# Moving the denominators' transfers to GpSimd, loading values last, and forming key-value sums directly as feature by value

## Chip, cores and metric

The kernel runs on one core of one Trainium2 chip. The metric is the device time of one execution in microseconds (us); lower is better. Three runs of the kernel before gave 923.36, 926.24 and 926.26 us, a median of 926.24 us.

## What is computed

The reference chains three parts; all data are float32 (some weights arrive as float64 words and are converted on the chip).

```python
def phi(x):                       # x: 4 batches, 8 heads, 576 tokens, 64 wide
    proj = x @ w_phi              # 128 features
    proj = proj - max(abs(proj), axis=-1)
    return concat(exp(proj), exp(-proj))
q_p, k_p = phi(q), phi(k)
kv  = einsum('bhsf,bhsd->bhfd', k_p, v)
z   = sum(k_p, axis=s)
out = einsum('bhsf,bhfd->bhsd', q_p, kv) / (einsum('bhsf,bhf->bhs', q_p, z) + 1e-6)
x = out as 2304 tokens x 512
h = max(x @ w1, x @ w2, x @ w3)   # 512 -> 768
y = h @ w_out                     # 768 -> 512
t = y @ w_in                      # 512 -> 2048
g = max(t, 0) + alpha * min(t, 0)
return g @ w_out2                 # 2048 -> 512
```

## The kernel before, in words

**Stages.** Heads are handled in pairs, 4 pairs a batch, 16 in all; pair number i counts through the batches. `keys(pair)` (L255) projects the keys, forms `e` = exp of both signs, and sums keys times values over five token tiles into one PSUM bank `kvp`. The values come with a block of ones between the two heads (`v`, shaped 5 x 3 x 64), so numerators and denominators come out of one product. `queries(pair)` (L313) projects the queries, transposes them, takes exp, multiplies by the pair's sums (`pn`), and copies numerator and denominator to `nd`. Then (L363 to L387) eight transfers a pair handle the denominators: two gather a denominator row into `dc` (64 partitions by 9), one moves the second head's numerators under the first's (`nd<-nd`), one writes the reciprocals to DRAM (`r_d`), four read them back broadcast (`xr<-r_d`). The product `xr` is split into a high and a low part (`xh`, `xl`), as every operand of the later matrix products is: a product is formed as three matmuls, high*high, high*low, low*high. For the first batch GpSimd does the multiply, the copy and the subtraction (L379 to L386); for others VectorE and ScalarE do.

**Plain pairs.** For the first two batches (8 pairs, `plain_kv`) the key-value sum is a plain float32 matmul, which the trace shows as two records each. It is formed value by feature: `rv` (128 columns) is loaded as weights and `e` streams 256 columns, so 10 matmuls a pair. The result is copied to `kvs` by ScalarE (L295), turned by four transposes on TensorE (L298) into `kvt`, and copied again to `kvf` (L301).

**Layer 1** (`layer1`, L398) works in units of one batch half (288 tokens) by 128 outputs: 36 matmuls, then ScalarE and VectorE take the maximum of three banks into `ho`, which goes to DRAM as `h_d` (L417). Units are placed between the pairs: unit number u0 = 3 * (i - 4) - LAG at pair i (L443), so that they fill TensorE during the attention; what is left runs after it (L538). `split_w123` converts their weights on VectorE and ScalarE (L153).

**Layer 2** (L548 to L563) reads `h_d` chunk by chunk (`load_h`, L516, tile `hr`) and writes `y_d` by way of `yo` (L560, two buffers). **Layer 3** (L608 to L634) reads `y_d`, writes `g_d`. **The last stage** (L642 to L683) goes through 9 blocks of 256 tokens, two halves each. It uses a seven-product scheme: `left(block, half)` (L582) reads `g_d` into `a`, forms four sums `s`, and makes seven factors `o` (high part by ScalarE, low part by L602: every second one on GpSimd except in the first block's first half, the others on VectorE). 168 matmuls a block take them in `ORDER`.

**What sets the order.** Each engine and each DMA queue works strictly in the order in which its instructions were laid down. That order comes from a planner that runs through a simulated timeline when the kernel is built, with the priorities that `tc.high_priority` gives. The loads of q, k, v and tails (L144), the staging of weights (L173, L468), the eight denominator transfers (L366, L367, L371, L378) and `h_d` of the first three batches all share SyncE's queue (SP); an instruction there that waits for a semaphore holds up those behind it. `g_d`, and `h_d` of the last batch, go by GpSimd's queue (POOL), `y_d` by ScalarE's.

Of the kernel before, what the change touches and what calls it, by code (L numbers as in the profile page):

```python
# [10 lines left out]
F32 = mybir.dt.float32  # L11
# [8 lines left out]
P = 128  # L20
# [13 lines left out]
CHUNKS = ((0, 2 * P), (2 * P, S - 2 * P))  # L34
EPS = 1e-6
XBUFS = (6, 6)
LAG = 1
PLAIN = 5
CONVERT_IN = (2, 1, 2, 1, 3, 3, 3, 3)
SOON, NOW, LATER, LAST = 400, 1000, -100, -200  # L40
# [11 lines left out]
def tile_kernel(ctx: ExitStack, tc: tile.TileContext, qT, kT, tails, v, w_phi, w1, w2, w3, w_out, w_in, w_out2, alpha, out):  # L52
# [82 lines left out]
    def load_pair(pair):  # L135

        odd = pair[1] % 2
        tags = ["xh", "rv", "rt", "xl"] if plain(pair) else ["raw", "rv", "rt", "raw"]
        if plain_kv(pair):
            tags[1] = ("vl", "vh")[odd]  # L140
        shapes = ([P, SM], [P, 5, 3, D], [P, 2 * ST], [P, SM])
        for what, tag, shape, src in zip("kvtq", tags, shapes, (kT, v, tails, qT)):
            t = ap.tile(shape, F32, tag=tag, bufs=2 if tag in ("raw", "xh", "xl") else 1, name=what)
            nc.sync.dma_start(t, src[pair])  # L144
            raws[pair, what] = t

    def plain(pair):
        return pair[0] * NPAIR + pair[1] < PLAIN

    def plain_kv(pair):  # L150
        return pair[0] < 2
# [103 lines left out]
    def keys(pair):  # L255

        rv = raws[pair, "v"]
        if not plain_kv(pair):
            if not vs:
                vs.extend(ap.tile([P, 5, 3, D], F32R, tag=tag, bufs=1, name=tag) for tag in ("vh", "vl"))  # L260
                part = slice(None)
            else:
                part = slice(None, None, 2)
            vh, vl = vs
            hi_act(vh[:, :, part], rv[:, :, part])
            sub(V, vl[:, :, part], rv[:, :, part], vh[:, :, part])
        kvp = bank("kv", 1, "kvp")
        first = True
        for tiles, e in exp_keys(pair):
            n = len(tiles) * 512  # L270
            if plain_kv(pair):
                ops = ((rv, e),)
            else:
                kh = ap.tile([P, 1024], F32R, tag="kh", bufs=2, name="kh")
                kl = ap.tile([P, 1024], F32R, tag="kl", bufs=2, name="kl")
                hi_act(kh[:, :n], e[:, :n])
                sub(V, kl[:, :n], e[:, :n], kh[:, :n])
                ops = ((vh, kh), (vl, kh), (vh, kl))
            yield
            for i, t in enumerate(tiles):  # L280
                for h in range(2):
                    c = slice(i * 512 + h * 256, i * 512 + h * 256 + 256)
                    for x, y in ops:
                        nc.tensor.matmul(  # L284
                            kvp[:, h * 256 : h * 256 + 256],
                            x[:, t, h : h + 2].rearrange("p a d -> p (a d)"),
                            y[:, c],
                            start=first,
                            stop=t == 4 and y is ops[-1][1],
                            skip_group_check=True,  # L290
                        )
                        first = False
        yield
        kvs = ap.tile([P, 512], F32, tag="kvs", bufs=1, name="kvs")
        A.activation(kvs, kvp, AF.Copy)  # L295
        kvt = bank("p1", 3, "kvt") if pair[0] == 0 else bank("kv", 1, "kvt")
        for i in range(4):
            nc.tensor.transpose(kvt[:, i * P : (i + 1) * P], kvs[:, i * P : (i + 1) * P], ident)  # L298
        if plain_kv(pair):
            kvf = ap.tile([P, 2, 2, P], F32, tag=("kvh", "kvl")[pair[1] % 2], bufs=2, name="kvf")  # L300
            A.activation(kvf.rearrange("p a b c -> p (a b c)"), kvt, AF.Copy)  # L301
            kvs_of[pair] = (kvf,)
            return
        kvh = ap.tile([P, 2, 2, P], F32R, tag="kvh", bufs=2, name="kvh")
        kvl = ap.tile([P, 2, 2, P], F32R, tag="kvl", bufs=2, name="kvl")
        hi_act(kvh.rearrange("p a b c -> p (a b c)"), kvt)
        sub(V, kvl.rearrange("p a b c -> p (a b c)"), kvt, kvh.rearrange("p a b c -> p (a b c)"))
        kvs_of[pair] = (kvh, kvl)
# [4 lines left out]
    def queries(pair):  # L313
# [49 lines left out]
        dc = ap.tile([P, S // D], F32, tag="dc", bufs=2, name="dc")  # L363
        for h in range(2):
            dr = D * (1 - h)
            nc.sync.dma_start(dc[h * D : (h + 1) * D], nd[h][dr : dr + 1].rearrange("a (p n) -> a p n", p=D))  # L366
        nc.sync.dma_start(nd[0][D:], nd[1][D:])  # L367
        V.tensor_scalar(dc, dc, EPS, None, op0=ALU.add)
        V.reciprocal(dc, dc)
        rows = r_d[pair[0], pair[1]]  # L370
        nc.sync.dma_start(rows.rearrange("h (p n) -> (h p) n", p=D), dc)  # L371
        res = []
        for c in range(2):
            cs = slice(c * CH, (c + 1) * CH)
            xr = raw_tile()
            for h in range(2):
                r = slice(h * D, (h + 1) * D)
                nc.sync.dma_start(xr[r], rows[h : h + 1, cs].to_broadcast([D, CH]))  # L378
            e = G if pair[0] == 0 else V  # L379
            e.tensor_tensor(xr, nd[0][:, cs], xr, op=ALU.mult)  # L380
            xh, xl = x_tiles(c)
            if pair[0] == 0:
                G.tensor_copy(xh, xr)  # L383
            else:
                hi_act(xh, xr)
            sub(e, xl, xr, xh)  # L386
            res.append((xh, xl))  # L387
# [10 lines left out]
    def layer1(b, c, f, x, w, spread=False):  # L398
        pw = []
        for j in range(3):  # L400
            if spread:
                p = bank(("pn", "pt", "kv")[j], 1, "p1")
            else:
                p = bank("p1", 3, "p1")
            ops = []
            for k in range(KT):
                ks = slice(k * P, (k + 1) * P)
                ops += three(w[j][:, 0, ks], w[j][:, 1, ks], *x[k][c])
            products(p[:, :CH], ops)
            pw.append(p)  # L410
        s1 = xp.tile([P, CH], F32, tag="s1", bufs=2, name="s1")
        A.activation(s1, pw[0][:, :CH], AF.Copy)
        V.tensor_tensor(s1, pw[1][:, :CH], s1, op=ALU.max)
        ho = xp.tile([P, CH], F32, tag="ho", bufs=2, name="ho")
        V.tensor_tensor(ho, pw[2][:, :CH], s1, op=ALU.max)  # L415
        o = b * S + c * CH
        (nc.gpsimd if b == B - 1 else nc.sync).dma_start(h_d[f, :, o : o + CH], ho)  # L417

    pairs = [(b, pr) for b in range(B) for pr in range(NPAIR)]
    xs = {b: [] for b in range(B)}  # L420
# [94 lines left out]

    def load_h(c, k):  # L516
        hh, hl = x_tiles(max(c % 2, k // XBUFS[0]))
        pool, tag, bufs = ((xp, "xr", 3), (xp, "xr", 3), (xp, "s1", 2), (gp, "neg", 2))[(2 * c + k) % 4]
        if c == 0:
            pool, tag, bufs = xp, "xr", 3  # L520
        hr = pool.tile([P, CH], F32, tag=tag, bufs=bufs, name="hr")
        nc.sync.dma_start(hr, h_d[k, :, c * CH : (c + 1) * CH])
        hi_act(hh, hr)
        sub(V, hl, hr, hh)
        hs[c, k] = (hh, hl)
# [22 lines left out]
    for c in range(2 * B):  # L548
# [5 lines left out]
        for m in range(KT):  # L554
            ms = slice(m * P, (m + 1) * P)
            ops = []
            for k in range(NF1):
                ops += three(wo[k][:, 0, ms], wo[k][:, 1, ms], *hs[c, k])
            products(p2[m][:, :CH], ops)
            yo = xp.tile([P, CH], F32, tag="ho", bufs=2, name="yo")  # L560
            A.activation(yo, p2[m][:, :CH], AF.Copy)
            nc.scalar.dma_start(y_d[m, :, t0 : t0 + CH], yo)
        convert(2)  # L563
# [13 lines left out]
    T = P  # L577
# [4 lines left out]
    def left(block, half):  # L582

        ready[block, half] = res = {}
        a = []
        for kh in range(2):
            t = ap4.tile([P, 4, 2 * T], F32, tag="a", bufs=4, name="a")
            r = slice(kh * 8 + half * 4, kh * 8 + half * 4 + 4)
            nc.sync.dma_start(t, g_d[r, :, block * 2 * T : (block + 1) * 2 * T].rearrange("f p n -> p f n"))
            a.append(t)  # L590
        (a00, a10), (a01, a11) = ((t[:, :, :T], t[:, :, T:]) for t in a)
        s1, s2, s3, s4 = (ap4.tile([P, 4, T], F32, tag="s", bufs=4, name="s") for _ in range(4))
        V.tensor_tensor(s3, a00, a10, op=ALU.subtract)
        V.tensor_tensor(s1, a10, a11, op=ALU.add)
        V.tensor_tensor(s2, s1, a00, op=ALU.subtract)
        V.tensor_tensor(s4, a01, s2, op=ALU.subtract)  # L596
        for n, i in enumerate(ORDER):
            src = (a00, a01, s4, a11, s1, s2, s3)[i]
            o = op4.tile([P, 2, 512], F32R, name="o") if half else ring2.tile([P, 2, 512], F32R, tag="w", name="o")
            ov = o.rearrange("p a (f n) -> p a f n", f=4)  # L600
            hi_act(ov[:, 0], src)
            sub(G if n % 2 and block + half else V, ov[:, 1], src, ov[:, 0])  # L602
            res[i] = o
            yield

    V.tensor_scalar(al, al, -1.0, 1.0, op0=ALU.mult, op1=ALU.add)
    load_y(0, 0)
# [129 lines left out]
```

## Time and profile before

| what | before |
|---|---|
| median of 3 runs | 926.24 us (923.36 to 926.26) |
| the profiled execution's own time | 925.09 us |
| its span, first to last instruction | 923.3 us |
| TensorE matmul busy | 899.8 us (97%), 6689 matmul records |
| VectorE busy | 642.5 us (70%) |
| ScalarE busy | 468.2 us (51%) |
| GpSimd busy | 173.5 us (19%) |
| mean granted TensorE clock | 0.997 |

In the profile's rows PE is TensorE's matmuls, PEld its weight loads, DVE VectorE, ACT ScalarE, POOL GpSimd and SP SyncE; SPq, POOLq and ACTq are these engines' DMA issues. A name like `p<-xh,w123t` says which tile is written from which. L253 and L74 are lines of helpers that all products and all low-part subtractions share. Matmul ends are modelled, so that overlapping matmuls count as busy while nothing is lost between them; starts are recorded.

### The profile page before, as it was taken

Reading aid. Unit: us, or ns where it says so; the run is one execution under the profiler, and the core shown is the slowest. Engines: PE = TensorE matmul, PEld = TensorE weight load, DVE = VectorE, ACT = ScalarE, POOL = GpSimd, SP = SyncE. Lnnn points to the kernel's source line nnn. Section 1 sums busy time; section 2 is a strip of 40 time slices with the busy share of each in tenths; the row PEclk is TensorE's granted clock in tenths of the full one; section 3 lists DMA queues with packets and bytes.
Section 4 is the critical chain, followed back from the end, with each engine's and each line's share of the span. In section 5 each row is a group of like instructions: output and inputs, shape, how many; then the busy total and the mean of one; then the engine's idle time right before and its main releaser. Section 6 shows DMA issues by size and latency. Waiting matters only on the chain.

```text
span 923.3 us, 18029 instructions
## 1 busy us (share of the span) xinstructions
PE 899.8 (97%) x6689; PEld 876.6 (95%) x6689; DVE 642.5 (70%) x1239; ACT 468.2 (51%) x1084; POOL 173.5 (19%) x221
## 2 busy tenths in 40 slices
PE   8987999999999999999999999999999998999998
PEld 7866899999999999999999999999999998999998
DVE  6998556788887632889889294447443598878881
ACT  5867556777777521444466363335333353444440
POOL 0032100000000000001000023333333363444440
PEclk9999999999999999999999999999999999999999
DMA  9664323222331112766678555445542345443421
GB/s 318 195 193 143 84 59 81 74 80 82 104 95 44 31 58 65 225 184 213 203 231 248 185 171 167 131 147 175 193 149 100 111 116 156 135 141 116 138 69 46
DMA packets 83159, 125.98 MB, mean 136 GB/s; under 512 B 14208, under 2 KB 61952, under 8 KB 83072
## 3 DMA queue, kind: packets, MB, share of 16 engines
q1 hardware_dynamic: 71744, 99.47, 36.4%
q0 software_dynamic: 6720, 20.65, 6.2%
q10 hardware_dynamic: 4608, 4.72, 1.5%
q8 instruction: 52, 0.85, 0.4%
q14 instruction: 35, 0.29, 0.1%
HBM read 86.91 MB, written 35.46 MB: 133 GB/s over the span
## 4 chain that ended last, share of the span: by engine, by line
PE 73%; DVE 11%; DMA 8%; issue 3%; ACT 2%; SPq 0%; POOL 0%; ACTq 0%; DVEq 0%; POOLq 0%
PE p L253 43%; PE acc L656 12%; PE kvp L284 6%; PE pn L253 5%; PE pj L253 5%; DVE o L74 2%; DMA st<-in_w_out 2%; DMA y_d<-yo 2%; PE pt L346 2%; DMA hr<-h_d 1%; DVE wt L87 1%; DVE wt L89 1%; ACT o L68 1%; DVE xl L74 1%; DVE s L596 1%
## 5 line engine op out<-in xcount | busy, mean ns | idle before, releaser
L253 PE MATMUL p<-xh,w123t 128*128 128x288 f32 x1152 | 242.3, 298 | 3.2 <-POOL xh L383 3.1
L253 PE MATMUL p<-xh,wi 128*128 128x288 f32 x1024 | 203.9, 296 | 1.2 <-DVE g L627 1.2
L253 PEld LDWEIGHTS p<-xh,w123t 128*128 128x128 f32 x1152 | 187.1, 188 | 4.8 <-POOL xh L383 3.5
L656 PE MATMUL acc<-wq,o 128*128 128x256 f32 x1512 | 182.0, 282 | 3.6 <-DVE o L74 3.2
L656 PEld LDWEIGHTS acc<-wq,o 128*128 128x128 f32 x1512 | 179.9, 190 | 5.6 <-DVE o L74 5.1
L253 PE MATMUL p<-xl,w123t 128*128 128x288 f32 x576 | 171.4, 298 | 0.0
L253 PEld LDWEIGHTS p<-xh,wi 128*128 128x128 f32 x1024 | 163.2, 188 | 1.5 <-DVE g L627 1.5
L253 PE MATMUL p<-xl,wi 128*128 128x288 f32 x512 | 149.5, 293 | 0.0
L253 PEld LDWEIGHTS p<-xl,w123t 128*128 128x128 f32 x576 | 108.2, 188 | 0.6
L628 POOL DMA_DIRECT2D g_d<-g x128 | 69.5, 544 | 208.5 <-DVE g L627 204.6
L627 DVE SCALAR_TENSOR_TENSOR g<-neg,al,p 128x288 f32<-128x288 f32 x128 | 64.3, 511 | 63.7 <-ACT neg L625 63.3
L253 PEld LDWEIGHTS p<-xl,wi 128*128 128x128 f32 x512 | 97.0, 190 | 0.0
L625 ACT ACTIVATE neg<-p 128x288 f32<-128x288 f32 x128 | 51.2, 407 | 84.9 <-PE p L253 81.0
L253 PE MATMUL p<-xh,wo 128*128 128x288 f32 x384 | 76.9, 296 | 0.8 <-ACT xh L68 0.7
L417 POOL DMA_DIRECT2D h_d<-ho x12 | 6.7, 555 | 354.7 <-DVE ho L415 354.7
L68 ACT ACTIVATE o<-s 128x512 fp32r<-128x512 f32 x72 | 44.3, 629 | 55.1 <-PE acc L656 29.6
L74 DVE TENSOR_TENSOR xl<-xr,xh 128x288 fp32r<-128x288 f32 x88 | 38.8, 455 | 37.2 <-ACT xh L68 32.2
L68 ACT ACTIVATE xh<-xr 128x288 fp32r<-128x288 f32 x88 | 37.8, 444 | 49.5 <-DMA xr<-y_d 34.3
L253 PEld LDWEIGHTS p<-xh,wo 128*128 128x128 f32 x384 | 61.1, 188 | 1.3 <-ACT xh L68 1.3
L74 POOL TENSOR_TENSOR o<-s,o 128x512 fp32r<-128x512 f32 x34 | 49.3, 1453 | 65.1 <-ACT o L68 65.1
L204 DVE TENSOR_REDUCE mx<-pj 128x4 f32<-128x512 f32 (+1 forms) x80 | 49.8, 627 | 10.6 <-PE pj L253 10.5
L253 PE MATMUL p<-xl,wo 128*128 128x288 f32 x192 | 56.3, 293 | 0.5 <-DVE xl L74 0.3
(138 smaller groups left out, 1632.3 us busy)
## 6 DMA issues: line engine op xcount, KB each, us to landing
g_d<-g POOLq DMA_DIRECT2D x128, 144.0 KB, 2.1
a<-g_d SPq DMA_DIRECT2D x36, 512.0 KB, 3.8
st<-in_w_out SPq DMA_DIRECT2D x22, 512.0 KB, 4.4
wst<-in_w SPq DMA_DIRECT2D x18, 512.0 KB, 5.6
xr<-y_d SPq DMA_DIRECT2D x64, 144.0 KB, 2.4
st<-in_w_in SPq DMA_DIRECT2D x16, 512.0 KB, 3.8
v<-in_v SPq DMA_DIRECT2D x16, 480.0 KB, 4.2
hr<-h_d SPq DMA_DIRECT2D x48, 144.0 KB, 3.9
```

Of the source, the lines that this page charges most:

```text
L68: A.activation(dst, src, AF.Copy)
L74: eng.tensor_tensor(dst, src, hi.bitcast(F32), op=ALU.subtract)
L87: V.scalar_tensor_tensor(wu, low, 29, wu, op0=ALU.logical_shift_right, op1=ALU.bitwise_or)
L89: V.scalar_tensor_tensor(wu, high, 0xC0000000, wu, op0=ALU.bitwise_and, op1=ALU.bitwise_or)
L204: V.tensor_reduce(mx, pv, axis=AX.X, op=ALU.max, apply_absolute_value=True, negate=True)
L253: nc.tensor.matmul(dst, x, y, start=i == 0, stop=i == len(ops) - 1, **kw)
L284: nc.tensor.matmul(kvp[:, h * 256 : h * 256 + 256], x[:, t, h : h + 2].rearrange("p a d -> p (a d)"), y[:, c], start=first, stop=t == 4 an ...
L346: nc.tensor.transpose(pt[:, c : c + P], pp[:, 2 * i + h], ident)
L625: A.activation(neg, p, AF.Relu, scale=-1.0)
L627: V.scalar_tensor_tensor(g, neg, al[:, f : f + 1], p, op0=ALU.mult, op1=ALU.add)
L628: nc.gpsimd.dma_start(g_d[f, :, c * CH : (c + 1) * CH], g)
L656: nc.tensor.matmul(acc[i], x, y, start=half == 0 and f == 0 and n == 0 and PLACE[i][1] == 0, stop=half == 1 and f == 3 and n == 2, skip_gr ...
```

## The change

`LAG` goes from 1 to 2. From the second pair on, a pair's loads go out in the order keys, tails, queries, values (before: keys, values, tails, queries). The eight denominator transfers and all `h_d` writes go by GpSimd's queue. The fourth pair's multiply and split go from GpSimd to VectorE and ScalarE. For the 8 plain pairs the key-value sum is formed feature by value: `e` is the weights, `rv` streams 128 columns, 20 matmuls a pair instead of 10, and the first copy and the transposes go away. `hr` uses the tags `xr` and `s1` alone (before also `neg`), `yo` uses `ho` and `neg` in turn (four buffers instead of two). In the last stage both halves of `a` are one tile, the sums `s` are formed between the factors instead of ahead of them, and every low part is made by VectorE.

```diff
-LAG = 1
+LAG = 2
...
-        for what, tag, shape, src in zip("kvtq", tags, shapes, (kT, v, tails, qT)):
+        for what, tag, shape, src in sorted(zip("kvtq", tags, shapes, (kT, v, tails, qT)), key=lambda x: ("ktqv" if i_of(pair) else "kvtq").index(x[0])):
...
-            for i, t in enumerate(tiles):
+            for i, t in enumerate(tiles if plain_kv(pair) else ()):
+                for j in range(4):
+                    c = slice(i * 512 + j * P, i * 512 + j * P + P)
+                    nc.tensor.matmul(
+                        kvp[:, j * P : (j + 1) * P],
+                        e[:, c],
+                        rv[:, t, j // 2 : j // 2 + 2].rearrange("p a d -> p (a d)"),
+                        start=first,
+                        stop=t == 4,
+                        skip_group_check=True,
+                    )
+                    first = False
+            for i, t in enumerate(() if plain_kv(pair) else tiles):
...
+        if plain_kv(pair):
+            kvf = ap.tile([P, 2, 2, P], F32, tag=("kvh", "kvl")[pair[1] % 2], bufs=2, name="kvf")
+            A.activation(kvf.rearrange("p a b c -> p (a b c)"), kvp, AF.Copy)
+            kvs_of[pair] = (kvf,)
+            return
         kvs = ap.tile([P, 512], F32, tag="kvs", bufs=1, name="kvs")
         A.activation(kvs, kvp, AF.Copy)
...
-            nc.sync.dma_start(dc[h * D : (h + 1) * D], nd[h][dr : dr + 1].rearrange("a (p n) -> a p n", p=D))
-        nc.sync.dma_start(nd[0][D:], nd[1][D:])
+            nc.gpsimd.dma_start(dc[h * D : (h + 1) * D], nd[h][dr : dr + 1].rearrange("a (p n) -> a p n", p=D))
+        nc.gpsimd.dma_start(nd[0][D:], nd[1][D:])
...
-        nc.sync.dma_start(rows.rearrange("h (p n) -> (h p) n", p=D), dc)
+        nc.gpsimd.dma_start(rows.rearrange("h (p n) -> (h p) n", p=D), dc)
...
-                nc.sync.dma_start(xr[r], rows[h : h + 1, cs].to_broadcast([D, CH]))
-            e = G if pair[0] == 0 else V
+                nc.gpsimd.dma_start(xr[r], rows[h : h + 1, cs].to_broadcast([D, CH]))
+            e = G if i_of(pair) < NPAIR - 1 else V
...
-        (nc.gpsimd if b == B - 1 else nc.sync).dma_start(h_d[f, :, o : o + CH], ho)
+        nc.gpsimd.dma_start(h_d[f, :, o : o + CH], ho)
...
-        pool, tag, bufs = ((xp, "xr", 3), (xp, "xr", 3), (xp, "s1", 2), (gp, "neg", 2))[(2 * c + k) % 4]
-        if c == 0:
-            pool, tag, bufs = xp, "xr", 3
+        tag, bufs = ("s1", 2) if c and k % 2 else ("xr", 3)
...
-            yo = xp.tile([P, CH], F32, tag="ho", bufs=2, name="yo")
+            pool, tag = ((xp, "ho"), (gp, "neg"))[m % 2]
+            yo = pool.tile([P, CH], F32, tag=tag, bufs=2, name="yo")
...
-            sub(G if n % 2 and block + half else V, ov[:, 1], src, ov[:, 0])
+            sub(V, ov[:, 1], src, ov[:, 0])
```

In `left` the new order is: factor 0, sums s1 and s2, factor 5, sum s3, factors 6, 4, 1, 3, sum s4, factor 2.

## Rows read from the trace of the kernel before

**Rows 1.** Busy time by stage: stretch, its length, then each engine's busy us.
```profile
core 0: us, PE busy (x) PEld busy (x) DVE busy (x) ACT busy (x) POOL busy (x), PEclk, DMA share, GB/s
0.00:100.00 100.00, 86.96 (x432) 72.19 (x433) 84.03 (x174) 68.00 (x159) 20.43 (x30) 1.00 0.63 199
100.00:360.00 260.00, 259.92 (x1966) 255.36 (x1965) 173.89 (x355) 158.15 (x408) 0.00 (x0) 1.00 0.26 72
...
460.00:540.00 80.00, 77.46 (x575) 76.11 (x575) 57.68 (x122) 46.11 (x113) 1.25 (x2) 1.00 0.69 213
...
735.00:770.00 35.00, 31.71 (x251) 30.90 (x250) 29.22 (x38) 15.64 (x29) 15.87 (x11) 0.95 0.48 139
770.00:904.00 134.00, 133.67 (x1127) 132.45 (x1126) 108.72 (x154) 61.17 (x102) 61.24 (x41) 1.00 0.40 119
```

**Rows 2.** Waits of PE in the first 100 us: total us, times, longest.
```profile
PE p L253 <- POOL xh L383: 3.1, 1, 3.1
PE pj L253 <- ACT ke L235: 3.0, 2, 2.7
```

**Rows 3.** Waits of DVE in the first 100 us.
```profile
DVE xht L71 <- DMA t<-in_tails: 3.4, 1, 3.4
DVE dc L368 <- DMA dc<-nd: 2.0, 1, 2.0
```

**Rows 4.** SP's issues in order of time: start, us, line, transfer.
```profile
69.53 1.10 SPq L378 DMA_DIRECT2D xr<-r_d  x2
70.68 0.58 SPq L144 DMA_DIRECT2D t<-in_tails  x1
```

**Rows 5.** Waits of the SP queue, 8 to 100 us.
```profile
SPq L378 <- DMA r_d<-dc: 12.3, 4, 4.2
```

**Rows 6.** POOL in order of time: first and last instruction of the fourth pair.
```profile
91.40 1.59 POOL L380 TENSOR_TENSOR xr<-nd,xr 128x288 f32<-128x288 f32 x1 [12.33 <-DMA xr<-r_d]
...
95.44 0.81 POOL L74 TENSOR_TENSOR xl<-xr,xh 128x288 fp32r<-128x288 f32 x1
```

**Rows 7.** The chain of waits, second plain pair: start, us, engine, tile, records.
```profile
31.51 0.44 PE kvt L298 x4
31.95 1.73 PE kvp L284 x8
```

**Rows 8.** Weight loads of the plain products, all: count, busy us, mean ns.
```profile
L284 PEld LDWEIGHTS kvp<-ke,v 128*128 128x128 f32 x160 | 29.6, 192 | 5.9 <-ACT ke L228 1.8 <-ACT ke L235 0.2
```

**Rows 9.** Idle time ahead of the instructions that touch yo: until what, us, times.
```profile
  DMA y_d<-yo: 19.2, 11
```

**Rows 10.** Waits of PE from 450 to 545 us.
```profile
PE p L253 <- DVE g L627: 1.2, 1, 1.2
```

**Rows 11.** A transfer's count, KB and us to landing.
```profile
hr<-h_d SPq DMA_DIRECT2D x48, 144.0 KB, 3.9
```

**Rows 12.** Waits of PE from 735 to 790 us.
```profile
PE acc L656 <- DVE o L74: 3.2, 2, 2.9
```

**Rows 13.** Groups from 785 to 885 us (five blocks): count, busy us, mean ns.
```profile
L74 POOL TENSOR_TENSOR o<-s,o 128x512 fp32r<-128x512 f32 x20 | 28.6, 1432 | 36.5 <-ACT o L68 36.5
...
L74 DVE TENSOR_TENSOR o<-a,o 128x512 fp32r<-128x512 f32 x20 | 20.6, 1032 | 3.4 <-ACT o L68 3.4
...
L74 DVE TENSOR_TENSOR o<-s,o 128x512 fp32r<-128x512 f32 x20 | 16.8, 839 | 12.8 <-ACT o L68 12.8
L594 DVE TENSOR_TENSOR s<-a 128x512 f32<-128x512 f32 x10 | 12.3, 1233 | 0.0
...
L595 DVE TENSOR_TENSOR s<-s,a 128x512 f32<-128x512 f32 x10 | 6.8, 678 | 0.0
```

**Rows 14.** Issues of transfers: count, ns shortest/median/longest, first and last start.
```profile
L628 POOL DMA_DIRECT2D g_d<-g x128: 539/539/867, 538.1 to 735.0; - x128
...
L417 SPq DMA_DIRECT2D h_d<-ho x36: 319/332/1037, 100.1 to 401.2; - x36
```

More of the change, by code (lines that the diff above doesn't have):

```diff
@@ L147, in plain, with i_of @@
     def plain(pair):
-        return pair[0] * NPAIR + pair[1] < PLAIN
+        return i_of(pair) < PLAIN
+    def i_of(pair):
+        return pair[0] * NPAIR + pair[1]
     def plain_kv(pair):
@@ L270, in keys @@
             n = len(tiles) * 512
-            if plain_kv(pair):
-                ops = ((rv, e),)
-            else:
+            if not plain_kv(pair):
                 kh = ap.tile([P, 1024], F32R, tag="kh", bufs=2, name="kh")
@@ L293, in keys @@
         yield
+        if plain_kv(pair):
[3 more added lines that the diff above has]
+            return
         kvs = ap.tile([P, 512], F32, tag="kvs", bufs=1, name="kvs")
         A.activation(kvs, kvp, AF.Copy)
-        kvt = bank("p1", 3, "kvt") if pair[0] == 0 else bank("kv", 1, "kvt")
+        kvt = bank("kv", 1, "kvt")
         for i in range(4):
             nc.tensor.transpose(kvt[:, i * P : (i + 1) * P], kvs[:, i * P : (i + 1) * P], ident)
[L299 to L303, printed above, removed]
         kvh = ap.tile([P, 2, 2, P], F32R, tag="kvh", bufs=2, name="kvh")
@@ L377, in queries @@
                 r = slice(h * D, (h + 1) * D)
-                nc.sync.dma_start(xr[r], rows[h : h + 1, cs].to_broadcast([D, CH]))
-            e = G if pair[0] == 0 else V
+                nc.gpsimd.dma_start(xr[r], rows[h : h + 1, cs].to_broadcast([D, CH]))
+            e = G if i_of(pair) < NPAIR - 1 else V
             e.tensor_tensor(xr, nd[0][:, cs], xr, op=ALU.mult)
             xh, xl = x_tiles(c)
-            if pair[0] == 0:
+            if e is G:
                 G.tensor_copy(xh, xr)
@@ L517, in load_h @@
         hh, hl = x_tiles(max(c % 2, k // XBUFS[0]))
-        pool, tag, bufs = ((xp, "xr", 3), (xp, "xr", 3), (xp, "s1", 2), (gp, "neg", 2))[(2 * c + k) % 4]
-        if c == 0:
-            pool, tag, bufs = xp, "xr", 3
-        hr = pool.tile([P, CH], F32, tag=tag, bufs=bufs, name="hr")
+        tag, bufs = ("s1", 2) if c and k % 2 else ("xr", 3)
+        hr = xp.tile([P, CH], F32, tag=tag, bufs=bufs, name="hr")
         nc.sync.dma_start(hr, h_d[k, :, c * CH : (c + 1) * CH])
@@ L584, in left, with factor @@
         ready[block, half] = res = {}
-        a = []
+        a = ap4.tile([P, 2, 4, 2 * T], F32, tag="a", bufs=2, name="a")
         for kh in range(2):
-            t = ap4.tile([P, 4, 2 * T], F32, tag="a", bufs=4, name="a")
             r = slice(kh * 8 + half * 4, kh * 8 + half * 4 + 4)
-            nc.sync.dma_start(t, g_d[r, :, block * 2 * T : (block + 1) * 2 * T].rearrange("f p n -> p f n"))
-            a.append(t)
-        (a00, a10), (a01, a11) = ((t[:, :, :T], t[:, :, T:]) for t in a)
+            nc.sync.dma_start(a[:, kh], g_d[r, :, block * 2 * T : (block + 1) * 2 * T].rearrange("f p n -> p f n"))
+        (a00, a10), (a01, a11) = ((a[:, kh, :, :T], a[:, kh, :, T:]) for kh in range(2))
         s1, s2, s3, s4 = (ap4.tile([P, 4, T], F32, tag="s", bufs=4, name="s") for _ in range(4))
[L593 to L598, printed above, removed]
+        def factor(i, src):
             o = op4.tile([P, 2, 512], F32R, name="o") if half else ring2.tile([P, 2, 512], F32R, tag="w", name="o")
@@ L601, in left @@
             hi_act(ov[:, 0], src)
-            sub(G if n % 2 and block + half else V, ov[:, 1], src, ov[:, 0])
+            sub(V, ov[:, 1], src, ov[:, 0])
             res[i] = o
-            yield
+        factor(0, a00)
+        V.tensor_tensor(s1, a10, a11, op=ALU.add)
+        V.tensor_tensor(s2, s1, a00, op=ALU.subtract)
+        yield
+        factor(5, s2)
+        V.tensor_tensor(s3, a00, a10, op=ALU.subtract)
+        yield
+        factor(6, s3)
+        yield
+        factor(4, s1)
+        yield
+        factor(1, a01)
+        yield
+        factor(3, a11)
+        V.tensor_tensor(s4, a01, s2, op=ALU.subtract)
+        yield
+        factor(2, s4)
     V.tensor_scalar(al, al, -1.0, 1.0, op0=ALU.mult, op1=ALU.add)
```

## The prediction

> **What bounds the kernel now.** I read the busy time by stage first. From 100 to 360 us and from 770 to 904 us TensorE has a matmul in flight all but 0.1 and 0.3 us of the time, at a granted clock of 1.00, the full 2.4 GHz [rows 1]. Nothing that other engines save can shorten these stretches; only less work on TensorE can. The reader is to look for the stretches where PE falls short of their length: 13.0 us of the first 100 (100 - 86.96), 2.5 us from 460 to 540, 3.3 us from 735 to 770. In the last one the mean clock is 0.95 as well, so some of it ran at 1.2 GHz, which is worth 0.05 x 35 = 1.8 us of full clock; TensorE had stood idle just before it dropped. So some 13 + 2.5 + 5.1 = 20.6 us lie open.
>
> The waits come next. In the first 100 us VectorE is busy 84 us, so it nearly sets the pace itself [rows 1]. Its largest wait for data is 3.4 us for the tails; it also loses 2.0 us to a denominator's transfer [rows 3]. The tails were issued at 70.68 us on SP, right behind two `xr` reads that began at 69.53 [rows 4], and the queue's own waits show what such reads hold back: 12.3 us in four waits for `r_d` to land [rows 5]. TensorE loses 3.1 us to the fourth pair's `xh`, made by GpSimd, and 3.0 us to key exponentials [rows 2].
>
> **The change part by part**, against the profiled execution's 925.1 us (span 923.3 and 1.8 around it). The median of three runs is 926.2, 1.1 above it; I carry the difference over to the median.
>
> *Queues, load order, LAG, and the fourth pair's split: -4.4 us.* With the eight denominator transfers on POOL, SP carries loads and nothing that waits for arithmetic before them, and the tails no longer stand behind `r_d`. I take the 3.4 us of VectorE back, since VectorE paces this stage. The fourth pair's multiply and split run from 91.40 to 96.25 us on GpSimd, 4.85 us [rows 6]. VectorE needs at most 0.678 us for each of its four (that row's 512 columns against 288 here [rows 13]), 2.7 us in all, besides two copies that ScalarE makes. So `xh` comes some 2 us earlier, but VectorE has up to 2.7 us more to do; TensorE's 3.1 us wait then shrinks, net, by perhaps 1 us. LAG moves one unit of layer 1 from this place to behind the attention. It adds no work, and it keeps that unit from standing at the head of TensorE's order while `xh` is still missing; I price it at nothing by itself, since the gain is already in the 1 us. The new queue costs GpSimd 0.539 us an issue against 0.332 on SP [rows 14], eight a pair, 4.3 us in place of 2.7; between 100 and 360 us GpSimd is idle (0.00), which covers it [rows 1]. If that cover goes, `ho` is late next (below). Loading values last puts the transfer that waits for the previous sums' last reader behind those that do not; that is part of the same 3.4 us. Bounds: all four waits of [rows 2, 3] gone, -11.5; nothing gained and VectorE's 2.7 us in full, +2.7. The value lies nearer the small end because VectorE's own 84 us stay.
>
> *Key-value sums as feature by value: -1.4 us.* Four transposes a pair go; four take 0.44 us in the chain, 0.11 each. The plain products take 1.73 us for eight records, 0.216 each [rows 7]. Ten matmuls are 20 records, 4.32 us. The new form has 40 records of half the columns: 40 x 0.108 = 4.32 by columns, 40 x 0.11 = 4.40 by the transposes, which also have 128 columns and also load new weights each time. I take the second, a net of 4.40 - 4.32 - 0.44 = -0.36 a pair. Only the second batch's four pairs lie where TensorE is full, so 4 x 0.36 = 1.4 us; the first four lie where VectorE paces. ScalarE's first copy also goes, on an engine with time to spare (158 of 260 us [rows 1]). Bounds: -0.44 x 8 = -3.5 if the products themselves cost nothing more; and if each weight load's 192 ns [rows 8] were no longer covered, 40 x 0.192 - 4.32 - 0.44 = +2.9 a pair, +23 for eight. The transposes at 0.11 are the nearest row and speak against that.
>
> *Buffers of `yo` and `hr`: -1.5 us.* ScalarE stands 19.2 us in 11 waits for a `y_d` write to free one of two `yo` buffers [rows 9], and what stands behind it in its order are high parts and the first evacuations of layer 3: TensorE's largest wait there, 1.2 us, is for that first `g` [rows 10]. Four buffers take most of ScalarE's wait away. Against it `hr` falls from seven buffers to five, with 3.9 us to landing [rows 11]. Bounds: all 2.5 us of the stage, or one such landing exposed, +3.9. I take rather more than the 1.2.
>
> *The last stage: -3.0 us.* All low parts move to VectorE: six of 14 a block. GpSimd's take 1.432 us each. While GpSimd runs, VectorE's own subtractions take 1.032 and 0.839 us on the mean and an `s` 1.233, against 0.678 for the `s` that meets none [rows 13]. So six operations of about 0.68, +4.1 us a block, are set against what the contention adds: 4 x 0.35 + 4 x 0.16 + 2 x 0.55 for L594 and as much or a little less for L593, some 4 us. VectorE stays at about 108.7 / 134 x 20 = 16.2 us of a 20 us block [rows 1]; the steady state does not move, and TensorE covers it. What moves is the start, where TensorE waits 3.2 us for a low part [rows 12] and pays 1.8 us of clock. The factor needed first now waits for no sum, and no factor waits 1.4 us for GpSimd. I take 3.0 of 5.1. Bounds: -5.1; +3.2, if VectorE with all 14 falls behind once more. The joined tile `a` is freed later, but there are still two; nothing.
>
> **Sum:** -4.4 - 1.4 - 1.5 - 3.0 = -10.3, so 914.8 for a profiled execution and 926.2 - 10.3 = 915.9 for the median: **916 us**.
>
> **Rivals.** *More comes back.* If the first 100 us are paced by waits and VectorE's work is mostly filler pulled forward (the weight conversions), all 11.5 us of [rows 2, 3] go instead of 4.4, and the last stage gives 5.1 instead of 3: 916 - 7.1 - 2.1 = 907. For it: the transfers lie one behind the other on SP; against: VectorE's 84%. Chance 0.17.
>
> *The early stage does not move*, because VectorE paces it whatever the queues do or because the planner lays the order differently from what the lines suggest: 916 + 4.4 = 920. For it: 84 of 100 us; against: 3.4 us of plain waiting for a load. Chance 0.17.
>
> *GpSimd's queue becomes late: slower.* The denominators and `h_d` now stand in one strict order on POOL. A `xr` read waits 12.3 / 4 = 3.1 us for `r_d` [rows 5], and eight issues take 4.3 us; an `h_d` behind them frees `ho` late, VectorE's maximum stands, and TensorE's banks stay full. It decides when `h_d` is held longer than the other `ho` buffer covers, one unit of 36 matmuls at 260 / 1966 = 0.132 us [rows 1], 4.8 us. 3.1 alone is under that, 3.1 + 4.3 is over. Were half of 3.1 us lost at each of the twelve later pairs, that is 18.6 us, and without the early gain: 926.2 + 18.6 - 1.4 - 1.5 - 3.0 = 939. Against it: before, the same transfers stood in one queue, SP's, with the loads besides, and from 100 to 360 us TensorE lost 0.1 us. The longest POOL issue is 0.867 us against 0.539 [rows 14], 0.33 more. Chance 0.10. The Trainium skill, in "SBUF — State Buffer", SBUF: two separate sides, says that descriptors of transfers issued from GpSimd are written through the port pair shared with VectorE, and that VectorE's two-port operations lock GpSimd out. Its example is a transfer that goes from 620 to 3100 ns; by that, an estimate, eight transfers would lose up to 8 x 2.5 = 20 us a pair, and this rival would be certain. The trace bears out a stretch of 0.33 us, not 2.5.
>
> **How the numbers follow.** The forecast's own case (911 to 920) has 0.48, more comes back 0.17 (904 to 911), the early stage unmoved 0.17 (920 to 924), a late POOL queue or uncovered weight loads 0.10 (over 929), and 0.08 for parts that cancel (924 to 929). A measurement of this kernel tells about 0.3%, 2.8 us, from no change. Faster by more than that, under 923.4: 0.48 + 0.17 + 0.16 = 0.81; within: 0.09; slower: 0.10. The range 906 to 924 leaves out the last two cases and the lower edge of the second, some 0.2.
>
> **What would show it.** Right: no DVE wait for the tails in the first 100 us, PE busy there over 90; no `kvt` records, `kvp` records 320 at 0.11 us; ScalarE's wait for `y_d` nearly gone; no GpSimd subtraction after 735 us, VectorE's at 0.68, PE's clock 1.00 there and its wait under 1 us. Wrong: a PE wait behind POOL issues or `ho` between 100 and 360 us, `kvp` starts over 0.15 us apart, or a DVE-bound block over 20.0 us.

## The result, and the profile after

The changed kernel takes 909.41 us (906.61 to 913.08, 4 runs) against 925.53 us (923.36 to 926.26, 4 runs) for the kernel before: a ratio of 0.983, 95% interval 0.981 to 0.986, or 16.1 us. The forecast was 916 us and a gain of 10.3. The two profiled executions below are 14.8 us apart.

The first and last start of each layer's matmuls tell where the time went. The columns are the line, count, shortest/median/longest ns, and first to last start in us. The kernel before:

```profile
L253 PE MATMUL p<-xh,wo x384: 293/296/399, 449.8 to 528.4; 128*128 128x288 f32 x192
...
L253 PE MATMUL p<-xh,wi x1024: 288/295/403, 528.6 to 733.5; 128*128 128x288 f32 x171
...
L656 PE MATMUL acc<-wq,o x1512: 274/280/580, 733.6 to 919.0; 128*128 128x256 f32 x189
```

The changed kernel:

```profile
L256 PE MATMUL p<-xh,wo x384: 293/297/442, 440.2 to 523.0; 128*128 128x288 f32 x192
...
L256 PE MATMUL p<-xh,wi x1024: 288/295/399, 523.1 to 726.8; 128*128 128x288 f32 x171
...
L679 PE MATMUL acc<-wq,o x1512: 274/280/286, 726.9 to 904.4; 128*128 128x256 f32 x189
```

Taken from one first start to the next, and to the end of the span (923.3 and 908.5 us):

| stage | before | after | difference |
|---|---|---|---|
| attention and layer 1, until layer 2's first matmul | 449.8 | 440.2 | -9.6 |
| layer 2 | 78.8 | 82.9 | +4.1 |
| layer 3 | 205.0 | 203.8 | -1.2 |
| last stage, to the end | 189.7 | 181.6 | -8.1 |

The busy time by stage after, to be held against [rows 1]:

```profile
0.00:100.00 100.00, 93.20 (x584) 81.89 (x585) 91.63 (x186) 69.76 (x167) 34.52 (x60) 1.00 0.66 208
100.00:360.00 260.00, 260.00 (x2011) 257.54 (x2010) 173.36 (x355) 156.26 (x399) 65.40 (x123) 1.00 0.25 71
...
735.00:770.00 35.00, 35.00 (x300) 35.00 (x300) 31.35 (x58) 16.76 (x30) 0.00 (x0) 1.00 0.37 117
770.00:904.00 134.00, 134.00 (x1144) 134.00 (x1143) 100.15 (x182) 54.66 (x93) 0.00 (x0) 1.00 0.39 122
```

In the first 100 us TensorE is busy 93.2 us in place of 87.0, so that it stands idle 6.8 us in place of 13.0. VectorE is busy 91.6 in place of 84.0: it was not full before. GpSimd carries 65.4 us of issues between 100 and 360 us, and TensorE loses nothing there. In the last stage GpSimd is gone, VectorE does all low parts in less busy time (100.2 us in 134 against 108.7), and TensorE gets more matmuls through: 300 in place of 251 from 735 to 770 us, and 1144 in place of 1127 from 770 to 904.

The largest waits of TensorE in the first 100 us after (total us, times, longest) are these. The 3.1 us for `xh` of [rows 2] is gone; for key exponentials (`ke`) 1.2 + 0.5 us are left of 3.0. VectorE's list of waits there has neither the tails nor `dc` of [rows 3].

```profile
PE warm L125 <- DVE signs L127: 1.5, 1, 1.5
PE kvp L284 <- ACT ke L238: 1.2, 2, 0.7
PE pj L256 <- issue: 1.1, 1, 1.1
PE pj L256 <- DMA k<-in_kT: 1.0, 1, 1.0
PE pn L256 <- ACT nd L348: 0.7, 1, 0.7
PE kvp L284 <- ACT ke L230: 0.5, 1, 0.5
```

The new products in the chain of waits after (start, us, records): 16 in 1.78 us, 0.111 us each, by [rows 7] half the time of the old ones.

```profile
17.16 1.78 PE kvp L284 x16
```

Layer 2 shows a wait that changed its name. ScalarE's longest waits there, before (450 to 529 us):

```profile
ACT yo L561 <- DMA y_d<-yo: 17.0, 10, 4.4
...
ACT xh L68 <- DMA hr<-h_d: 5.0, 3, 2.7
```

and after (440 to 525 us):

```profile
ACT xh L68 <- DMA hr<-h_d: 16.1, 11, 2.4
```

The wait for a `yo` buffer is gone, and almost as much has come up as a wait for `hr`.

### The profile page after: what moved, and what is told of

It is laid out like the page before. It is cut to its first block, busy times and chain, and to the rows that moved or that the text cites. A ratio compares the mean times of both kernels' runs of the same rounds, so it can differ in the third digit from the quotient of the medians.

```text
span 908.5 us, 18237 instructions
## 1 busy us (share of the span) xinstructions
PE 894.6 (98%) x6817; PEld 878.6 (97%) x6817; DVE 643.1 (71%) x1294; ACT 465.9 (51%) x1078; POOL 179.7 (20%) x328
## 4 chain that ended last, share of the span: by engine, by line
PE 80%; DVE 8%; DMA 8%; issue 2%; ACT 1%; SPq 0%; DVEq 0%; ACTq 0%
PE p L256 41%; PE acc L679 19%; PE pj L256 5%; PE pn L256 5%; DMA st<-in_w_in 3%; PE kvp L284 3%; PE kvp L297 3%; DMA st<-in_w_out 3%; DVE wt L89 2%; PE pt L359 2%; DVE wt L87 2%; DMA hr<-h_d 1%; ACT wt L81 1%; DVE wt L83 1%; DVE xl L74 1%
## 5 line engine op out<-in xcount | busy, mean ns | idle before, releaser
L256 PE MATMUL p<-xh,w123t 128*128 128x288 f32 x1152 | 239.9, 297 | 0.0
L679 PE MATMUL acc<-wq,o 128*128 128x256 f32 x1512 | 177.8, 280 | 0.0
L679 PEld LDWEIGHTS acc<-wq,o 128*128 128x128 f32 x1512 | 177.7, 188 | 0.0
L430 POOL DMA_DIRECT2D h_d<-ho x48 | 27.1, 565 | 154.4 <-DVE ho L428 147.7
L68 ACT ACTIVATE o<-a 128x512 fp32r<-128x512 f32 x54 | 33.6, 629 | 37.2 <-PE acc L679 24.6
```

The source lines that it names most:

```text
L68: A.activation(dst, src, AF.Copy)
L256: nc.tensor.matmul(dst, x, y, start=i == 0, stop=i == len(ops) - 1, **kw)
L430: nc.gpsimd.dma_start(h_d[f, :, o : o + CH], ho)
L679: nc.tensor.matmul(acc[i], x, y, start=half == 0 and f == 0 and n == 0 and PLACE[i][1] == 0, stop=half == 1 and f == 3 and n == 2, skip_gr ...
```

## The experiments

Each run below leaves one edit out of the changed kernel unless it says otherwise, so a loss is what that edit is worth beside all others. Ratios are to runs of the kernel before on the same chip in the same session (medians 924.2 to 924.4 us); the changed kernel's own is 0.983 (0.981 to 0.986). The medians of two kernels compared here can come from different chips. The stage times come from one profiled execution each: layer 2's first matmul lies between 440.1 and 442.3 us in the five kernels whose source is the same up to there (the changed kernel, e1 to e4), so 2.2 us in this mark tells nothing.

**Last stage, old routine (e1).**

```diff
-            sub(V, ov[:, 1], src, ov[:, 0])
+            sub(G if n % 2 and block + half else V, ov[:, 1], src, ov[:, 0])
```

with the old order of sums and two tiles for `a`.

> The changed kernel with the last stage's old factor routine: every second low part on GpSimd, sums ahead of the factors, two tiles for a. Theory: the last stage's gain of 8.1 us (189.7 us from its first matmul to the end before, 181.6 us after) comes from this routine alone. Then the stage takes 188 to 190 us again, TensorE's wait of some 3 us near its start is back, and the whole is some 8 us slower than the changed kernel, about 917 us. Rival: the gain comes from how the kernel arrives there (conversions done earlier, nothing left over from the layers before). Then the stage stays at 182 to 183 us and the whole near 909 us.

Measured 915.94 us, ratio 0.991 (0.989 to 0.994), and the stage takes 187.2 us (727.7 us to the end at 914.9). The waits of TensorE from 720 us on:

```profile
PE acc L668 <- DVE o L74: 3.1, 2, 2.9
```

The wait of [rows 12] is back, and the stage is 5.6 us longer. The rival falls. Of the 2.5 us that remain of the 8.1, an estimated 1.8 is what the profile before lost to the clock in this stage [rows 1]; e1's clock was 1.00 from 735 to 770 us. This stage repeats well: it takes 181.6 to 181.9 us in the eleven kernels here without GpSimd's low parts, and 187.2 (e1), 189.3 (e10) and 189.7 (before) in the three with them.

**Last stage, old order, all on VectorE (e2).** As e1, with `sub(V, ...)`.

> As the run before this one, but every low part on VectorE; only the old order of sums and factors and the two tiles for a are left. Theory: what counted is that GpSimd is gone, since VectorE's subtractions beside it took 0.84 to 1.03 us in place of 0.68. Then the stage takes 181.5 to 183 us. Rival: the order counted, since the first factor had to wait for four sums. Then a stall of 2 us or more stays at the start and the stage takes 184 to 187 us.

Measured 910.75 us, ratio 0.985 (0.981 to 0.989), stage 181.7 us (725.3 to 907.0): the whole gain. The order of sums and factors is worth nothing that can be seen. VectorE's groups from 770 to 870 us, in e1 and then in e2 (count, busy us, mean ns):

```profile
L74 DVE TENSOR_TENSOR o<-a,o 128x512 fp32r<-128x512 f32 x20 | 19.3, 963 | 4.3 <-ACT o L68 4.3
L74 DVE TENSOR_TENSOR o<-s,o 128x512 fp32r<-128x512 f32 x20 | 17.7, 884 | 12.6 <-ACT o L68 12.6
L605 DVE TENSOR_TENSOR s<-a 128x512 f32<-128x512 f32 x11 | 12.2, 1107 | 0.5
```

```profile
L74 DVE TENSOR_TENSOR o<-s,o 128x512 fp32r<-128x512 f32 x41 | 28.1, 689 | 12.7 <-ACT o L68 12.5
L74 DVE TENSOR_TENSOR o<-a,o 128x512 fp32r<-128x512 f32 x31 | 21.2, 685 | 2.1 <-ACT o L68 2.1
...
L605 DVE TENSOR_TENSOR s<-a 128x512 f32<-128x512 f32 x10 | 6.9, 688 | 0.2
```

Beside GpSimd the same instructions take 0.88 to 1.11 us, without it 0.69. The 30-odd subtractions that VectorE takes over in these five blocks cost it nothing, because the ones it already had become shorter. In e1 TensorE loses most of its time between 755 and 760 us, and VectorE is busy 4.97 of these 5 us. What the runs do not separate is VectorE's slower instructions from GpSimd's own low parts, of 1.3 to 1.9 us each: the same edit takes both away.

**Layer 2, buffers shared otherwise (e3).**

```diff
-        tag, bufs = ("s1", 2) if c and k % 2 else ("xr", 3)
-        hr = xp.tile([P, CH], F32, tag=tag, bufs=bufs, name="hr")
+        pool, tag, bufs = ((xp, "xr", 3), (xp, "s1", 2))[k % 2 if c else 0]
+        if c and k == NF1 - 1:
+            pool, tag, bufs = gp, "neg", 2
+        hr = pool.tile([P, CH], F32, tag=tag, bufs=bufs, name="hr")
...
-            pool, tag = ((xp, "ho"), (gp, "neg"))[m % 2]
+            pool, tag = ((xp, "ho"), (gp, "neg"))[m == KT - 1]
```

> The changed kernel with the buffers of layer 2 shared out otherwise: hr takes neg for the last of its six tiles (six or seven buffers in turn instead of five), yo takes neg for one of its four tiles instead of two. Theory: layer 2 went from 78.8 to 82.9 us because hr lost two buffers, and yo's wait of 17 us on ScalarE was worth less. Then giving hr a sixth tile's buffer brings layer 2 to 78 to 81 us and the whole 2 to 4 us under the changed kernel. Rival: layer 2 became longer for another reason (h_d's landing, conversions of weights that now fall there). Then it stays at 82 to 84 us.

Measured 909.67 us, ratio 0.984 (0.980 to 0.987): no different from the changed kernel, although layer 2 took 79.5 us in the profile; layer 3 took 206.0. Whether 79.5 means anything the next run tells.

**Layer 2, buffers of before (e4).**

```diff
-        tag, bufs = ("s1", 2) if c and k % 2 else ("xr", 3)
-        hr = xp.tile([P, CH], F32, tag=tag, bufs=bufs, name="hr")
+        pool, tag, bufs = ((xp, "xr", 3), (xp, "xr", 3), (xp, "s1", 2), (gp, "neg", 2))[(2 * c + k) % 4]
+        if c == 0:
+            pool, tag, bufs = xp, "xr", 3
+        hr = pool.tile([P, CH], F32, tag=tag, bufs=bufs, name="hr")
...
-            pool, tag = ((xp, "ho"), (gp, "neg"))[m % 2]
-            yo = pool.tile([P, CH], F32, tag=tag, bufs=2, name="yo")
+            yo = xp.tile([P, CH], F32, tag="ho", bufs=2, name="yo")
```

> The changed kernel with hr and yo in the buffers of before: seven for hr, two for yo. Theory: the buffers set layer 2. Then it takes 78 to 80 us, ScalarE waits some 17 us for y_d again and 5 us in place of 16 for hr, and the whole is some 3 to 4 us under the changed kernel, about 905 to 906 us. Rival: the longer layer 2 is work or transfers that slid into it from the stages ahead. Then it stays at 82 to 84 us whatever the buffers.

Measured 911.44 us, ratio 0.987 (0.982 to 0.991), layer 2 81.0 us. ScalarE's waits did swap back as expected (440 to 525 us):

```profile
ACT yo L574 <- DMA y_d<-yo: 23.6, 15, 3.6
...
ACT xh L68 <- DMA hr<-h_d: 4.5, 4, 2.8
```

but the time did not follow. The theory that the buffers made layer 2 longer falls. The nine other kernels that share the changed kernel's layer 2 (e1, e2, e5 to e9, e11, e12) spread from 79.1 to 82.0 us around a mean of 80.3, so the 82.9 of the first profile was its upper end. The edit exchanges two waits of the same size. The whole is 2.0 us slower than the changed kernel by the medians, with intervals that overlap, and its layer 2 lies inside that spread; the edit is worth nothing that these runs can tell.

**Transfers back on SP (e5).** All `nc.gpsimd.dma_start` of the denominators, and `h_d` of the first three batches, as `nc.sync.dma_start`.

> The changed kernel with the eight denominator transfers and h_d of the first three batches back on SP. Theory: of the 9.6 us that the part up to layer 2 gained (449.8 to 440.2 us until layer 2's first matmul) the queues are the larger part, because loads no longer stand behind r_d. Then layer 2 begins at 445 to 449 us, VectorE waits 2 us or more for a load in the first 100 us, and the whole is 5 to 8 us slower than the changed kernel. Rival: the products' new form, LAG or the load order did it, and the queues cost nothing that TensorE feels. Then layer 2 begins at 440 to 442 us.

Measured 911.41 us, ratio 0.987 (0.983 to 0.991); layer 2 begins at 443.1 us, 2.9 later. VectorE's waits for these transfers in the first 100 us:

```profile
DVE dc L381 <- DMA dc<-nd: 3.3, 3, 2.4
DVE xr L393 <- DMA xr<-r_d: 1.7, 2, 1.0
...
DVE xht L71 <- DMA t<-in_tails: 1.0, 1, 1.0
```

It lies between the two: the waits for denominators and tails do come back, and TensorE is busy 90.9 of the first 100 us against 92.6 to 93.2 in the five kernels with the transfers on GpSimd and the same source up to layer 2. The mark of 443.1 us is 0.8 us beyond the latest of those five. In the whole time it is 2.0 us by the medians and 3.6 by the ratios, with intervals that overlap, no more than for e4: that the queues are worth some 2 us is likely and not shown.

**Key-value sums value by feature (e6).** The loop of products and the copy, transposes and copy of the kernel before.

> The changed kernel with the plain key-value sums formed value by feature again, with the copy and the four transposes. Theory: TensorE's own work is what counts, 0.36 us a pair and only for the four pairs in the full stretch, so layer 2 begins 1.4 us later, at 441 to 443 us. Rival: in the first 100 us the shorter way from kvp to kvf (no copy and no transposes, on ScalarE and TensorE) let every pair follow sooner. Then it begins 4 us later or more, at 444 us and over.

Measured 917.03 us, ratio 0.992 (0.989 to 0.995), 7.6 us slower than the changed kernel, and layer 2 begins at 449.6 us, as late as before. The rival holds, and by more than it asked for. Busy time by stage:

```profile
0.00:100.00 100.00, 89.14 (x427) 72.47 (x428) 89.89 (x179) 68.94 (x161) 31.67 (x57) 0.98 0.60 199
100.00:360.00 260.00, 260.00 (x1974) 256.07 (x1974) 173.46 (x355) 159.62 (x409) 66.08 (x122) 1.00 0.25 72
```

TensorE is full from 100 us on in both; what differs is how much work is behind it by then. The 9.4 us between the two marks can be estimated from rows: TensorE's own work at the prediction's price, 8 pairs of 0.36 us, 2.9; its idle time in the first 100 us, 10.9 against 6.8, 4.1; and the clock, 0.98 against 1.00, some 2. That is 9.0. The run says as much of the other edits: without the new products, the queues, the load order, LAG and the fourth pair together leave layer 2's start where it was (449.6 against 449.8).

**Old load order (e8).** The plain `zip("kvtq", ...)`.

> The changed kernel with the loads in the old order, keys, values, tails, queries. Theory: values wait for the last reader of the sums two pairs earlier and hold up tails and queries on SP, so part of the early gain hangs on this. Then layer 2 begins 1 to 4 us later, at 441 to 444 us, and VectorE or TensorE waits for tails or queries in the first 100 us. Rival: with the denominators gone from SP the queue has time to spare. Then it begins within 1 us of 440.2 us.

Measured 909.85 us, ratio 0.984 (0.980 to 0.988); layer 2 begins at 441.1 us. The rival: nothing that can be told.

**Fourth pair on GpSimd (e9).**

```diff
-            e = G if i_of(pair) < NPAIR - 1 else V
+            e = G if pair[0] == 0 else V
...
-            if e is G:
+            if pair[0] == 0:
```

> The changed kernel with the fourth pair's multiply and split on GpSimd again. Theory: the second unit of layer 1 begins when the fourth pair is ready, and GpSimd takes some 2 us longer for it, of which 1 us is felt: layer 2 begins at 440.5 to 442 us, with a wait of TensorE or its weight loads for GpSimd's xh near 95 us. Rival: with the transfers in front of it in GpSimd's queue this is late by far more, 3 us or over, and layer 2 begins at 443 us or later.

Measured 910.28 us, ratio 0.984 (0.980 to 0.987). Layer 2 begins at 443.7 us in the profile, as the rival had it and 1.4 us beyond the spread of the mark, but the median is only 0.9 us up, and no wait for `xh` stands in TensorE's list from 60 to 110 us. Inconclusive.

**LAG back at 1 (e7).**

> The changed kernel with LAG back at 1. Theory: LAG moves a unit of layer 1 without adding work, so layer 2 begins within 1.5 us of 440.2 us. Rival: the unit stands at the head of TensorE's order while the fourth pair's xh is missing, and TensorE waits 2 us or more for it near 90 us; then layer 2 begins at 442 us or later.

Measured 908.07 us, ratio 0.982 (0.980 to 0.984); layer 2 begins at 441.8 us. LAG is worth nothing that can be told.

**The key-value edit alone, in the kernel before (e10).**

> The kernel before with one edit: the plain key-value sums formed feature by value, without the copy and the transposes. With the old form put back into the changed kernel, layer 2 began at 449.6 us, as late as before. Theory: this edit carries the early gain by itself. Then layer 2 begins at 440 to 444 us and the whole is 6 to 9 us under the kernel before. Rival: it gives that much only together with the other edits of the attention (transfers on GpSimd above all). Then layer 2 begins at 446 us or later and the whole is 1 to 4 us under.

Measured 922.99 us, ratio 0.999 (0.997 to 1.000), 1.3 us, not clear of noise. In this build the planner put layer 2's first matmuls ahead of layer 1's last, so layer 3's first is the mark: 530.3 us, against 528.6 before. Busy time by stage, and TensorE's waits in the first 100 us:

```profile
0.00:100.00 100.00, 88.28 (x510) 77.49 (x510) 80.68 (x162) 62.87 (x148) 21.29 (x30) 0.93 0.63 199
```

```profile
PE pj L253 <- DVE pp L208: 3.2, 2, 1.8
PE p L253 <- POOL xh L393: 2.6, 1, 2.6
```

The rival holds in time: alone, the edit gives little. TensorE again stands before the fourth pair's `xh`, as in [rows 2]; its idle time in this stretch is 11.7 us, only 1.3 less than before; and the granted clock falls to a mean of 0.93, an estimate of 7 us that the profile before did not lose. Over the runs the difference in clock is smaller, 0.992 against 0.994 by the medians, 0.002 x 924 = 1.8 us. So the 1.3 us mixes the edit with the clock: it would be some 3 at equal clocks, still under 7.6. Which of the other edits it needs was not shown; e5 and e9 undo the two nearest, one at a time, and lose 2.0 and 0.9 us by the medians.

**Products and way on, crossed (e11, e12).** e11 has the new products and the old way on from `kvp`; e12 the old products and the new way on. Both leave out that the sums come out the right way round.

> The changed kernel with the 20 products of 128 columns kept, but the old way on from kvp put back for the plain pairs: copy to kvs, four transposes, copy to kvf. The sums of these pairs come out turned, so this part of the computation is changed. Theory: the gain of the new form is the shorter way on (a copy by ScalarE, four transposes and the waits between them, and a bank of PSUM), so layer 2 begins at 446 to 450 us. Rival: the gain lies in the products themselves, which let TensorE start on a quarter of e and take it in smaller pieces. Then it begins at 440 to 442 us.

Measured 912.06 us, ratio 0.987 (0.985 to 0.989), layer 2 at 445.4 us.

> The changed kernel with the 10 products of 256 columns put back for the plain pairs, but the short way on kept: one copy from kvp to kvf, no transposes. The sums of these pairs come out turned, so this part of the computation is changed. Theory: the way on is what counts, so layer 2 begins at 439 to 442 us, as with the change. Rival: the products count, and it begins at 446 us or later.

Measured 912.75 us, ratio 0.989 (0.986 to 0.992), layer 2 at 443.8 us, with a mean clock of 0.97 in the first 100 us, worth 3 us. Neither half gives the whole and neither gives nothing: of the 7.6 us between e6 and the changed kernel the new products (e11) bring 5.0 by the medians and 4.7 by the ratios, the new way on (e12) 4.3 and 2.2. The intervals of e12 and e6 overlap, and so do those of e11 and e12; which half weighs more stays open.

## Why the prediction was right, and where it was off

**Direction and range** held: the forecast was faster with 0.81 and 906 to 924 us. The time lies in the case called "more comes back" (904 to 911), not in the likeliest. Its reading of the early part was the better one: of the 11.5 us of waits in [rows 2, 3] all but 1.7 went. That the range held owes something to errors of opposite sign: by the profile the early part gave 9.6 where the terms had 5.8, and the last stage 8.1 where they had 3.0, but layer 2 lost 4.1 where 1.5 was to be gained.

**Key-value sums, -1.4 us: the term that was mis-sized.** Its price per record was right, 0.111 us against 0.11, and the weight loads of 0.19 us stayed covered. The step that failed is "only the second batch's four pairs lie where TensorE is full ... the first four lie where VectorE paces". Both halves are misread. Six of the eight pairs had their products in the first 100 us of the kernel before (120 of 160 records):

```profile
L284 PE MATMUL kvp<-ke,v 128*128 128x256 f32 x120 | 29.9, 387 | 0.3 <-ACT ke L228 0.3
```

And from 10 to 40 us TensorE was full there as well (30.00 of 30 us). VectorE was nearly so (28.22), but the chain of waits from 14 to 34 us holds TensorE alone:

```profile
by line: PE kvp L284 39.9%; PE pj L253 28.1%; PE pn L253 20.5%; PE pt L346 8.7%; PE kvt L298 4.4%
```

Put back, the old form costs 7.6 us (e6) and nearly the whole early gain, more than the 2.9 us of TensorE's own work in eight pairs. The rest is idle time of TensorE and clock, which the price per record cannot hold. That the edit shortens a chain of hand-overs in the first pairs fits this; no run takes the copy, the transposes and the hand-overs apart from one another. It is worth 7.6 us only beside the other edits: alone it gave 1.3 us (e10), and the others without it moved layer 2's start by 0.2 us (e6). I added up parts that need one another.

**VectorE paces: wrong for the stretch as a whole.** In the kernel before it stood idle 16 of the first 100 us. Its busy time in the first 100 us rose from 84.0 to 91.6 us. Of the 84.0, 50.9 were conversions of layer 1's weights, 54.0 of the 91.6; the first rival had suspected such work, though no run shows how much of it could have waited. In the changed kernel VectorE is busy without a gap from 60 to 100 us, so there it may pace.

**Queues, order, LAG and fourth pair, -4.4 us: the waits went, the worth was too large.** The wait for tails went, as did the one for GpSimd's `xh`. But by themselves these edits moved nothing (e6). Undone beside the new products, the queues cost 2.0 us by the medians, which the intervals do not tell from nothing; nor can order, LAG and the fourth pair be told from it.

**Buffers of layer 2, -1.5 us: nothing.** The step took ScalarE's 17 us of waiting as the thing to be saved and gave the loss of two `hr` buffers too little weight; the wait moved from one to the other.

**Last stage, -3.0 us: too small.** It measured 8.1 in the profile, and the run without the edit was 6.5 us slower by the medians (915.94 against 909.41). GpSimd was the cause, as written (e2). The start was worth more than the 5.1 us open there: from 735 to 770 us 49 more matmuls go through, 49 x 0.117 = 5.7 us. And the steady state also moves: from 770 to 904 us it is 17 more, 17 x 0.117 = 2.0 us, in a stretch where TensorE had a matmul in flight for 133.67 of 134 us. The prediction's reading that only less work on TensorE could shorten such a stretch was wrong. The argument that the factor must not wait for sums was wrong; e2 shows the old order to be as good.

**GpSimd's queue late: did not come.** 65.4 us of issues from 100 to 360 us, and TensorE lost nothing. Of the transfers that moved to POOL the longest `h_d` issue took 0.76 us, the longest `xr` read 0.64, the longest `r_d` write 0.78. The Trainium skill, "SBUF — State Buffer", SBUF: two separate sides, has transfers issued from GpSimd stretch to several times their length beside VectorE's two-port operations. Here VectorE was busy 91.6 of the first 100 us and no issue did, so the loss that the prediction estimated from the page did not come. Which of VectorE's operations here are such two-port ones no row shows; the page's example itself is not tested.

## What to carry to other kernels

Undo each part of a change in the finished version, and also try the promising one alone: here one edit was worth 7.6 us beside the others and 1.3 without them. A start-up stretch in which two engines are some 85% busy need not be paced by either: look at shorter slices for which one is full when, and expect an edit there to be worth more or less than the work it removes. An idle GpSimd is not free help for two-input VectorE work: the six subtractions a block that it took off VectorE cost VectorE as much as they saved. Know the spread of a stage's time before reading a difference in it: here the last stage repeats to 0.3 us, and layer 2 only to about 4.

## What the hardware showed that I had not expected

The clock may carry part of the gain. In 17 runs of the kernel before on the last chip the mean granted clock was 0.990 to 0.998; four runs of the changed kernel had 0.996 to 1.0 (913.08 us at 0.996, 906.61 at 1.0), and the four with LAG at 1 had 0.998 to 1.0. At a typical 0.994 against 0.999 that is an estimate of 0.005 x 924 = 4.6 us of full clock out of 16. But most of the gain is not clock: the two profiled executions had nearly the same mean, 0.997 and 0.998, and are still 14.8 us apart. A low clock goes with the idle stretches: in the profile before, the mean is 0.95 where TensorE waits at the start of the last stage [rows 1] and 1.00 there after, and the run with the early waits left in (e10) has 0.93 in its first 100 us against 1.00 after. What part of the 16 us is clock was not tried by itself.
